# Transposing the second product of an MLP block, building a mask once, and loading the next stage earlier in a fused attention and two-MLP kernel

## The chip, the core and the metric

One NeuronCore of one Trainium2 chip runs the whole program. The metric is device time in microseconds (us), the median of three runs. The engines are TensorE (PE in the profile; its weight loads are a row of their own, PEld), VectorE (DVE), ScalarE (ACT), GpSimd (POOL) and SyncE (SP), which here issues nearly all transfers.

## The reference, cut to what matters

```python
# q, k, v: (4, 8, 576, 64); f: (4, 8, 576); per MLP: w_in (512, 2048), w_out (2048, 512); all float32
scores = q @ k.T / 8 + (cum[:, None] - cum[None, :])      # cum = cumsum(log(clip(f)))
x = softmax(causal(scores)) @ v                           # heads joined: x is (2304, 512)
h = x @ w_in;  y = (h - tanh(h)) @ w_out                  # first MLP
h = y @ w2_in; out = maximum(h, 0) ** 2 @ w2_out          # second MLP
```

## The kernel before

**Number format.** Each float32 operand of the MLPs is kept as two fp32r tiles, a rounded part ("hi", index 0) and the rest ("lo", index 1). A product is three matmuls, listed in `PASSES`: hi by hi, hi by lo, lo by hi. `ghl` is the pair for the activations between the layers, `wout(fc, hl, lo, n)` the pair for 128 rows of `w_out`, of which it gives columns `lo` to `lo + n`.

**Order.** A stream of attention steps and a stream of first-MLP steps are interleaved by cost (the `Clockwork` object runs each step, and runs follow-up work, such as a conversion, a set number of steps later). A scheduler then orders each engine's queue by that program order and by when it expects operands. From the last MLP block on, many instructions are held to program order (`pin`, `move`).

**Attention sums.** The cumulative sums of `log f` are matmuls with a triangle of ones. `first_sums` builds that triangle on POOL in a tile `early("tri")`, and makes the sums for the first 256 positions. At slot 16 of the attention `more_sums` builds the triangle again in a buffer of the ring "g" (three buffers, also used for the MLP's tanh results `g1` and for `ys`), copies a 64x64 corner of it twice (`twice`), makes the sums of the later positions, and builds a causal mask, of which `mask4` keeps two corners.

**First MLP.** 2304 tokens are taken in seven blocks of 256 tokens (j = 0 to 6) and one last block of 512 (j = 7, `LAST`). A block of 256 takes 8 steps, each with two 128-wide chunks of the hidden layer; the last block takes 16 steps with one chunk each. A step has the products into `h` (line 1010), then tanh on ACT (1020), the subtraction on DVE (1023), hi on ACT (1027) and lo on DVE (1031). One step later `y1_atoms` adds that chunk's part to y (line 1050): the weights are the stationary operand and the activations stream through, so y comes out transposed, 128 model dimensions by tokens. For a block of 256 each of the four atoms of a step writes one half of a PSUM bank, with matmuls 256 columns wide: 24 to a step. When a block is done, `y1_out` copies its two banks `y0` and `y1` into `ys` (the first on DVE, the second on ACT) and stores each with one transfer to `yscr[j]`, which is laid out `[128, 4, 256]`.

**Weights of the second MLP.** During the last block the second MLP's `w_in` is loaded in eight pieces (line 140), unpacked (ACT 203 and 204, DVE 210 and 212), combined into sums on POOL (256) and split into hi and lo (ACT 312, DVE 313). A piece can only be loaded when the last block has used the weights that lie in its place.

**First stage of the second MLP.** It works on 768 tokens at a time. Its first third of y is read back from `yscr` by `first_y_load` (12 transfers, line 151) at step 6 of the last block; at step 8 `y_sums` queues four subtractions on POOL (line 1178); at steps 9 to 15 `y_split` makes one of seven hi and lo pairs each (ACT 1166, DVE 1167). After the last block come its products (`r`, line 1222) and then the second layer (`o`, line 1380).

Of the kernel before, what the change touches and what calls it, by code (L numbers as in the profile page):

```python
# [10 lines left out]
F32 = mybir.dt.float32  # L11
# [99 lines left out]
def fused_kernel(ctx: ExitStack, tc: tile.TileContext, q, k, v, f, w1i, w1o, w2i, w2o, out):  # L111
# [269 lines left out]
    def early(name):  # L381
        return m1.tile([P, 2, 512], F32, tag="ghl", name=name, bufs=2).rearrange("p a n -> p (a n)")[:, :S]

    def triangle(tri):
        nc.gpsimd.memset(tri, 1.0)
        nc.gpsimd.affine_select(tri[:, 0:P], tri[:, 0:P], pattern=[[1, P]], compare_op=ALU.is_ge,
                                fill=0.0, base=0, channel_multiplier=-1)
# [25 lines left out]
            nc.vector.tensor_scalar(ccol[:, t], cps[:, t * 32 : t * 32 + 32], 8.0, None, op0=ALU.mult)  # L413

    def first_sums():
        flog = early("flog")[: B * H]
        load(flog, f.rearrange("b h s -> (b h) s"))
        load_next("qk")
        load_next("v")
        load_next("qk")  # L420
        load_next("v")
        feed.upload(UP[0])
        make_identity(nc, ident)
        tri = early("tri")
        triangle(tri)
        nc.vector.tensor_scalar(flog, flog, 1e-4, 1.0, op0=ALU.max, op1=ALU.min)
        nc.scalar.activation(flog, flog, AF.Ln)
        nc.scalar.activation(st[0][: B * H, :1], flog[:, :1], AF.Exp)
        lps = bank("a", 4, "lps")
        for c, (k0, kn) in enumerate(KC):  # L430
            nc.tensor.transpose(lps[:kn, c * 32 : c * 32 + 32], flog[:, k0 : k0 + kn], ident[:32, :32])
        nc.vector.tensor_copy(lfT[:, 0:4], lps[:, 0:128].rearrange("p (c h) -> p c h", c=4))
        nc.vector.tensor_copy(lfT[:64, 4], lps[:64, 128:160])
        t = bank("a", 4, "neg0")
        for i in range(2):
            for c in range(2):
                k0, kn = KC[c]
                nc.tensor.matmul(t[:, 256 * i + k0 : 256 * i + 256], lhsT=lfT[:, c, i : i + 1].to_broadcast([P, P]),
                                 rhs=tri[:, : 256 - k0], start=c == 0, stop=c == 1)
        neg = ap.tile([P, S], F32, tag="neg", name="neg_0", bufs=2)  # L440
        nc.scalar.activation(neg[:, :512], t, AF.Copy, scale=-8.0)
        for i in range(2):
            negs[i] = neg[:, 256 * i : 256 * i + 256]
        sum_logs(0, tri, flog)

    def more_sums():
        row = m1.tile([P, 512], F32, tag="g", name="row1", bufs=3)
        tri = m1.tile([P, 512], F32, tag="g", name="tri1", bufs=3)
        triangle(tri)
        t = m1.tile([P, 512], F32, tag="g", name="mask1", bufs=3)  # L450
        m, twice = t[:, :P], t[:D, P : 2 * P]
        for x in range(2):
            nc.gpsimd.tensor_copy(twice[:, x * D : x * D + D], tri[:D, :D])
        sum_logs(1, tri, row[: B * H], twice)
        nc.gpsimd.memset(m, 0.0)
        nc.gpsimd.affine_select(m, m, pattern=[[-1, P]], compare_op=ALU.is_ge, fill=MASK, base=0, channel_multiplier=1)
        for x in (slice(0, D), slice(D, P)):
            nc.gpsimd.tensor_copy(mask4[x], m[x, x])

    units = [(b, hf, h) for hf in range(2) for b in range(B) for h in range(H)]  # L460
    NU = len(units)
# [140 lines left out]
            cw.later(LAG['qk'], lambda: nc.vector.tensor_copy(kq(n), t))  # L602
        return [(1024, a)]

    KLh = []
# [30 lines left out]
    def k_split(n):  # L636
        if not KLh:
            open_halves()
        r = raws.pop(("qk", n))[:, :S]
        for i in range(2):  # L640
            own = slice(i * D, i * D + D)
            split(r[own], K1[own, i, :], KLh[i][own, :])
        nc.sync.dma_start(K1[D : 2 * D, 0].bitcast(F32), K1[0:D, 0].bitcast(F32))
        nc.sync.dma_start(K1[0:D, 1].bitcast(F32), K1[D : 2 * D, 1].bitcast(F32))

    def softmax_of(i):

# [77 lines left out]
    def s_atom(i):  # L725

        n, ts = slots[i]
        hh = units[n][2] % 2

        def a():  # L730
            ti, rows, o, w = ts[0]
            parts = []
            for c0, m in ((0, w),) if w <= 512 else ((0, 288), (288, 288)):
                t = bank("a", 4, f"s_{i}_{c0}")
                todo = [(h, xt(n, h, q_cols(h, 4) - D * (1 - h), P)) for h in (1, 0)] if ti == 4 else [(hh, xt(n, hh, q_cols(hh, ti), P))]
                for x, (h, lhsT) in enumerate(todo):
                    nc.tensor.matmul(t[:, :m], lhsT=lhsT, rhs=K1[:, h, c0 : c0 + m], start=x == 0, stop=False)  # L737
# [296 lines left out]
        return [(6 * n, lambda i=i: a(i)) for i in range(len(todo))]  # L1034

    def y1_atoms(j, s):
        n = 512 if j == LAST else NB
        per = 512 // n
        end = s == n_steps(j) - 1

        def a(i):
            if s == 0 and i == 0:
                yb[j] = [bank("a", 4, f"y1_{j}_{m}") if j == LAST else bank(f"y{m}", 1, f"y1_{j}_{m}")
                         for m in range(ND // per)]
            ghl = gt[j, s]
            t = yb[j][i // per]
            o = t[:, (i % per) * n : (i % per) * n + n]
            for fj, fc in enumerate(chunks_of(j, s)):
                for wh, xh in PASSES:
                    nc.tensor.matmul(o, lhsT=wout(fc, wh, i * P, P), rhs=ghl[:, xh, fj * n : fj * n + n],  # L1050
                                     start=s == 0 and fj == 0 and wh + xh == 0 and i % per == 0,
                                     stop=end and fj == per - 1 and wh == 1, skip_group_check=True)
            if end and i % per == per - 1:
                cw.later(1, lambda: y1_out(j, i // per))

        return [(3 * per * n, lambda i=i: a(i)) for i in range(ND)]

    def y1_out(j, m):
        ys = m1.tile([P, 512], F32, tag="g", name=f"ys_{j}_{m}", bufs=3)
        (nc.scalar.copy if m % 2 else nc.vector.tensor_copy)(ys, yb[j][m])  # L1060
        if j == LAST:
            for o in range(2):
                nc.sync.dma_start(yscr[j + o][:, m, :], ys[:, o * NB : (o + 1) * NB])
        else:
            nc.sync.dma_start(yscr[j][:, 2 * m : 2 * m + 2, :], ys.rearrange("p (c n) -> p c n", c=2))

    def mlp1_stream():

# [2 lines left out]
        for i, (j, s) in enumerate(steps):  # L1071
# [87 lines left out]
    def y_quarter(dst, i, dh, th):  # L1159
        for b in range(3):  # L1160
            move(dst[:, :, b * P : (b + 1) * P],
                 yscr[3 * i + b][:, 2 * dh : 2 * dh + 2, th * P : (th + 1) * P])

    def y_split(i, k, src):
        t = y_tile(i, k)
# [14 lines left out]
    def y_sums(i):  # L1180
        for x in range(4):
            cw.later(2 * x, lambda x=x: y_sum(i, x))

    def first_y_load():
        m2 = box2["m2"]
# [356 lines left out]
```

## Time and profile before

| | |
|---|---|
| Median of three runs | 1023.09 us (1022.45 to 1023.16) |
| Profiled execution | 1020.46 us, of which 1018.7 us are the span from the first to the last instruction |
| Mean granted TensorE clock | 0.991 of full speed |
| Start of the kernel and attention alone | up to about 55 us |
| Attention with blocks 0 to 6 of the first MLP | to 530 us; block 6 ends at 559 us |
| Last block of 512 tokens | 553 to 655 us |
| Second MLP, first layer and second layer | 655 to 860 us, and from there to the end |

The profile is of a single execution, and its span is 1.8 us shorter than the execution's own time. Times given as positions are microseconds from the first instruction.

### The profile page before, as it was taken

What the parts mean: (1) busy time and instruction counts of PE and PEld (TensorE: products, weight loads), DVE (VectorE), ACT (ScalarE), POOL (GpSimd) and SP (SyncE); (2) the same over time, 40 slices, a digit from 0 to 9 for tenths busy, and PEclk for the clock granted to TensorE, in tenths of its full rate; (3) what the DMA queues carried; (4) which work ended last, traced back from release to release, by engine and by line L of the source; (5) the groups of instructions that cost most, each with busy time, mean ns of one, the idle gap of its engine ahead of it and who ended that gap; (6) DMA issues with size and microseconds to landing.
All of it is one profiled execution on the core that took longest, in us unless ns stands there. A gap on an engine that the chain in (4) does not pass through costs nothing.

```text
span 1018.7 us, 19954 instructions
## 1 busy us (share of the span) xinstructions
PE 987.6 (97%) x7022; PEld 939.2 (92%) x7022; DVE 717.8 (70%) x1497; ACT 628.7 (62%) x1249; POOL 350.5 (34%) x515
## 2 busy tenths in 40 slices
PE   7989999999999999999999989999999998999998
PEld 5778889999999999999999867899999998999998
DVE  4895974677877777877653488855447579887773
ACT  5895974566666665765643357767667776655551
POOL 3673642455465555555420163352232000000000
PEclk9997999999999999999999999999999999999999
DMA  8937655253353443443201532385977975444431
GB/s 236 274 125 220 206 122 114 71 138 74 90 135 83 100 114 91 110 103 85 68 14 37 155 109 98 109 286 198 307 255 265 299 245 147 145 135 135 124 105 42
DMA packets 217445, 146.97 MB, mean 144 GB/s; under 512 B 115872, under 2 KB 195040, under 8 KB 217344
## 3 DMA queue, kind: packets, MB, share of 16 engines
q1 hardware_dynamic: 217296, 145.65, 49.0%
q8 instruction: 55, 0.90, 0.4%
q14 instruction: 46, 0.38, 0.1%
q10 hardware_dynamic: 48, 0.03, 0.0%
HBM read 101.00 MB, written 39.92 MB: 138 GB/s over the span
## 4 chain that ended last, share of the span: by engine, by line
PE 74%; DVE 8%; issue 6%; ACT 5%; POOL 3%; DMA 3%; SPq 0%; ACTq 0%; DVEq 0%; POOLq 0%
PE h L1010 16%; PE o L1380 15%; PE r L1222 15%; PE y L1050 15%; PE pv L855 4%; PE pt L772 2%; PE s L737 2%; PE s L738 2%; PE pv L817 1%; POOL Pb L549 1%; DVE ghl L1031 1%; DVE g L1023 1%; POOL w L228 1%; DMA wraw<-in_moe_w_in_dram 1%; PE s L706 1%
## 5 line engine op out<-in xcount | busy, mean ns | idle before, releaser
L1050 PE MATMUL y<-ghl,w 128*128 128x256 f32 (+1 forms) x1536 | 244.3, 303 | 4.6 <-DVE ghl L1031 4.6
L1050 PEld LDWEIGHTS y<-ghl,w 128*128 128x128 f32 x1536 | 211.6, 192 | 18.4 <-DVE ghl L1031 6.5
L1010 PE MATMUL h<-x,w 128*128 128x256 f32 x1344 | 196.2, 289 | 5.6 <-POOL w L228 5.1
L1010 PEld LDWEIGHTS h<-x,w 128*128 128x128 f32 x1344 | 175.1, 192 | 10.0 <-POOL w L228 6.6
L1380 PE MATMUL o<-ws,gc 128*128 128x256 f32 x864 | 116.4, 283 | 0.0
L1380 PEld LDWEIGHTS o<-ws,gc 128*128 128x128 f32 x864 | 109.3, 192 | 0.0
L1222 PE MATMUL r<-yt,ws 128*128 128x384 f32 x576 | 106.0, 336 | 1.0 <-ACT g L1240 1.0
L1222 PEld LDWEIGHTS r<-yt,ws 128*128 128x128 f32 x576 | 100.0, 188 | 2.7 <-ACT g L1240 2.3
L1380 PE MATMUL o<-wq,gc 128*128 128x256 f32 x648 | 91.6, 284 | 3.1 <-DVE gc L1346 2.5
L256 POOL TENSOR_TENSOR wsum<-wfull 128x256 f32<-128x256 f32 x32 | 31.0, 969 | 167.1 <-DVE wfull L212 139.5
L1380 PEld LDWEIGHTS o<-wq,gc 128*128 128x128 f32 x648 | 83.7, 192 | 4.0 <-DVE gc L1346 3.1
L691 POOL TENSOR_SCALAR Pb<-Pb,st 128x384 f32<-128x384 f32 (+2 forms) x80 | 53.8, 672 | 97.2 <-DVE st L685 81.6
L1346 DVE TENSOR_TENSOR gc<-graw,gc 128x1792 fp32r<-128x1792 f32 x34 | 68.6, 2022 | 20.1 <-ACT gc L1345 20.0
L675 ACT ACTIVATE Pb<-Pb,st 128x384 f32<-128x384 f32 (+2 forms) x80 | 55.2, 690 | 43.8 <-DVE st L666 42.6
L1222 PE MATMUL r<-yt,wq 128*128 128x384 f32 x432 | 80.0, 335 | 0.3 <-ACT g L1240 0.2
L1023 DVE TENSOR_TENSOR g<-h,g 128x512 f32<-128x512 f32 x72 | 49.4, 686 | 42.6 <-ACT g L1020 41.4
L666 DVE CUSTOM_DVE_ANT_0 Pb<-s,Pb 128x128 f32<-128x128 f32 (+4 forms) x144 | 66.7, 479 | 17.7 <-PE s L738 12.2
L1222 PEld LDWEIGHTS r<-yt,wq 128*128 128x128 f32 x432 | 75.1, 188 | 1.3 <-ACT g L1240 1.2
L1345 ACT ACTIVATE gc<-graw 128x1792 fp32r<-128x1792 f32 x34 | 57.7, 1699 | 29.6 <-PE o L1380 17.1
L1020 ACT ACTIVATE g<-h 128x512 f32<-128x512 f32 x72 | 42.5, 590 | 46.1 <-PE h L1010 43.4
L782 DVE TENSOR_TENSOR PT<-pt,PT 128x512 fp32r<-128x512 f32 (+1 forms) x80 | 50.7, 634 | 26.4 <-ACT PT L781 23.1
L1233 DVE TENSOR_TENSOR g<-r,g 128x384 f32<-128x384 f32 x71 | 39.1, 553 | 41.6 <-PE r L1222 23.4
(162 smaller groups left out, 1895.7 us busy)
## 6 DMA issues: line engine op xcount, KB each, us to landing
graw<-gscr SPq DMA_DIRECT2D x144, 128.0 KB, 2.5
gscr<-g SPq DMA_DIRECT2D x95, 192.0 KB, 4.4
wraw<-in_moe_w_in_dram SPq DMA_DIRECT2D x32, 512.0 KB, 4.6
wraw<-in_moe_w_out_dram SPq DMA_DIRECT2D x32, 512.0 KB, 5.5
neg<-cscr SPq DMA_DIRECT2D x32, 288.0 KB, 3.7
v<-in_v_dram SPq DMA_DIRECT2D x48, 128.0 KB, 2.8
qk<-in_k_dram SPq DMA_DIRECT2D x64, 72.0 KB, 2.4
K<-K SPq DMA_DIRECT2D x32, 144.0 KB, 3.3
```

Of the source, the lines that this page charges most:

```text
L666: nc.vector.tensor_tensor_reduce(out=d, in0=t[:rows, src : src + m], in1=d, scale=-0.125, scalar=3.0e38 if j == 0 else stat(0, x)[:rows], ...
L675: nc.scalar.activation(d, d, AF.Exp, bias=stat(len(parts) - 1, x)[:rows], scale=-1.0, accum_out=stat(2, x)[:rows])
L691: nc.gpsimd.tensor_scalar(d, d, r, 1.0, op0=ALU.mult, op1=ALU.mult)
L782: cw.later(LAG['trlo'], lambda: nc.vector.tensor_tensor(dst[1], src, dst[0].bitcast(F32), op=ALU.subtract))
L1010: nc.tensor.matmul(o, lhsT=win(fc, wh, dc), rhs=xpart(j, dc, xh), start=dc == 0 and wh + xh == 0, stop=dc == ND - 1 and wh == 1)
L1020: pin(nc.scalar.activation(g, t, AF.Tanh))
L1023: pin(nc.vector.tensor_tensor(g, t, g, op=ALU.subtract))
L1050: nc.tensor.matmul(o, lhsT=wout(fc, wh, i * P, P), rhs=ghl[:, xh, fj * n : fj * n + n], start=s == 0 and fj == 0 and wh + xh == 0 and i % ...
L1222: nc.tensor.matmul(t, lhsT=wprod(1, p, k, wh)[:, dc * P : (dc + 1) * P], rhs=yt[i, k][:, xh, dc], start=k in FRESH and dc == 0 and wh + xh ...
L1345: pin(nc.scalar.activation(hi, t[:, 1:8], AF.Copy))
L1346: pin(nc.vector.tensor_tensor(lo, in0=t[:, 1:8], in1=hi.bitcast(F32), op=ALU.subtract))
L1380: nc.tensor.matmul(o, lhsT=gc[n][gh, e][:, GWHERE[k]] if n == 1 else gc[n][gh][:, GWHERE[k], e], rhs=wprod(2, 2 * q + e, k, wh), start=q = ...
```

## The change

Three edits are made together. The triangle and the mask are built once, in `first_sums`, in the memory that the attention's K tiles take later; `more_sums` uses them again. The second product of the blocks of 256 has its operands exchanged: a 128-token piece of the activations is stationary and 512 columns of `w_out` stream, so that y comes out as tokens by model dimensions, in half as many matmuls of twice the width. Both banks are then transposed in blocks of 32 by 32 on DVE and stored by four transfers each, with 128-byte runs, into a `yscr` that is now laid out `[512, 256]`. The last block keeps its form. The load, the sums and the splits for the second MLP's first stage are spread from step 1 of the last block on.

```diff
-    yscr = [dram.tile([P, ND, NB], F32, name=f"yscr_{j}") for j in range(NBLK)]
+    yscr = [dram.tile([DM, NB], F32, name=f"yscr_{j}") for j in range(NBLK)]
...
-    K1 = ap.tile([P, 2, S], F32R, name="K1")
-    KL = ap.tile([P, S], F32R, name="KL")
+    K1, KLh = [], []
+    early = [ap.tile([P, 2, S], F32, tag="K1", name="early0", bufs=1),
+             ap.tile([P, S], F32, tag="KL", name="early1", bufs=1)]
...
     def first_sums():
-        flog = early("flog")[: B * H]
+        flog = early[0][: B * H, 1]
...
-        tri = early("tri")
+        tri = early[0][:, 0]
         triangle(tri)
+        m, twice = early[1][:, :P], early[1][:D, P : 2 * P]
+        for x in range(2):
+            nc.gpsimd.tensor_copy(twice[:, x * D : x * D + D], tri[:D, :D])
+        nc.gpsimd.memset(m, 0.0)
+        nc.gpsimd.affine_select(m, m, pattern=[[-1, P]], compare_op=ALU.is_ge, fill=MASK, base=0, channel_multiplier=1)
+        for x in (slice(0, D), slice(D, P)):
+            nc.gpsimd.tensor_copy(mask4[x], m[x, x])
...
     def more_sums():
-        row = m1.tile([P, 512], F32, tag="g", name="row1", bufs=3)
-        tri = m1.tile([P, 512], F32, tag="g", name="tri1", bufs=3)
-        triangle(tri)
...     (the same copies, mask and corners as above, in a third buffer of "g")
+        sum_logs(1, early[0][:, 0], early[0][: B * H, 1], early[1][:D, P : 2 * P])
...
     def open_halves():
-        KLh.append(KL)
+        K1.append(ap.tile([P, 2, S], F32R, tag="K1", name="K1", bufs=1))
+        KLh.append(ap.tile([P, S], F32R, tag="KL", name="KL", bufs=1))
...
     def y1_atoms(j, s):
...
+        todo = [(m, fj, fc) for m in range(len(yb0[j])) for fj, fc in enumerate(chunks)]
...
+            for x, y in PASSES:
+                if j == LAST:
+                    l, r = wout(fc, x, m * P, P), ghl[:, y]
+                else:
+                    l, r = ghl[:, x, fj * NB + m * P : fj * NB + m * P + P], wout(fc, y)
+                nc.tensor.matmul(o, lhsT=l, rhs=r, start=s == 0 and fj == 0 and x + y == 0,
+                                 stop=end and fj == len(chunks) - 1 and x == 1)
...
     def y1_out(j, m):
         ys = m1.tile([P, 512], F32, tag="g", name=f"ys_{j}_{m}", bufs=3)
-        (nc.scalar.copy if m % 2 else nc.vector.tensor_copy)(ys, yb[j][m])
...
-            nc.sync.dma_start(yscr[j][:, 2 * m : 2 * m + 2, :], ys.rearrange("p (c n) -> p c n", c=2))
+        nc.vector.transpose(ys, yb[j][m])
+        for a in range(0, P, 32):
+            dst = yscr[j][:, m * P + a : m * P + a + 32].rearrange("(b j) t -> j b t", j=32)
+            nc.sync.dma_start(dst, ys[a : a + 32].rearrange("j (b t) -> j b t", t=32))
...
     def mlp1_stream():
-            if last and s == 6:
+            if last and s == 1:
                 yield 0, first_y_load, j
-            if last and s == 8:
-                yield 0, (lambda: y_sums(0)), j
-            if last and 9 <= s < 9 + len(SPLITS):
-                yield 0, (lambda s=s: y_split(0, SPLITS[s - 9], yraw[0][SPLITS[s - 9]])), j
+            if last and s in SUMMED:
+                yield 0, (lambda x=SUMMED.index(s): y_sum(0, x)), j
+            if last and s in SPLIT:
+                yield 0, (lambda k=SPLITS[SPLIT.index(s)]: y_split(0, k, yraw[0][k])), j
...
+    SUMMED, SPLIT = (3, 4, 6, 7), (5, 6, 8, 9, 11, 13, 15)
```

## Rows read from the trace of the kernel before

**Rows 1.** The page, busy time of each engine and its share.

```profile
PE 987.6 (97%) x7022; PEld 939.2 (92%) x7022; DVE 717.8 (70%) x1497; ACT 628.7 (62%) x1249; POOL 350.5 (34%) x515
```

**Rows 2.** Windows: length, busy time per engine, clock, DMA share, GB/s.

```profile
55.00:93.00 38.00, 33.81 (x201) 29.82 (x202) 26.93 (x59) 26.07 (x63) 19.51 (x26) 0.82 0.49 154
...
130.00:230.00 100.00, 98.61 (x808) 96.09 (x808) 66.31 (x180) 58.28 (x147) 40.80 (x74) 1.00 0.46 110
...
430.00:530.00 100.00, 99.02 (x783) 96.89 (x782) 70.41 (x187) 59.18 (x133) 48.74 (x79) 1.00 0.29 75
...
591.20:607.20 16.00, 12.33 (x49) 9.74 (x48) 13.12 (x14) 6.99 (x13) 11.39 (x8) 0.92 0.20 66
607.20:655.00 47.80, 46.85 (x208) 38.45 (x207) 41.95 (x60) 32.45 (x59) 19.98 (x19) 0.99 0.28 93
```

**Rows 3.** The chain that ended last: start, length, what.

```profile
544.62 2.88 PE y L1050 x24
...
553.26 2.75 PE h L1010 x12
...
577.95 2.72 PE y L1050 x12
...
647.97 4.18 PE r L1222 x24
...
654.91 65.07 PE r L1222 x372
```

**Rows 4.** Groups by shape, 130 to 561 us.

```profile
L1050 PE MATMUL y<-ghl,w 128*128 128x256 f32 x1196 | 171.2, 287 | 0.0
...
L1060 ACT COPY ys<-y 128x512 f32<-128x512 f32 x7 | 4.1, 586 | 5.3 <-PE y L1050 5.3
```

**Rows 5.** Groups by shape, whole span.

```profile
L1050 PE MATMUL y<-ghl,w 128*128 128x256 f32 x1344 | 195.5, 289 | 0.0
...
L634 DVE STREAM_TRANSPOSE qk<-qk 128x576 f32<-128x576 f32 x16 | 12.3, 771 | 0.2
...
L622 DVE STREAM_TRANSPOSE qk<-qk 128x320 f32<-128x320 f32 x16 | 8.1, 505 | 0.8 <-DMA qk<-in_q_dram 0.7
```

**Rows 6.** Waits of TensorE's weight loads, 130 to 553 us: total, times, longest.

```profile
PEld pv L855 <- ACT PT L781: 5.3, 14, 0.9
```

**Rows 7.** Transfers by source: count, KB each, us to landing.

```profile
qk<-in_k_dram SPq DMA_DIRECT2D x64, 72.0 KB, 2.4
...
yscr<-ys SPq DMA_DIRECT2D x14, 256.0 KB, 2.1
```

**Rows 8.** Timeline of POOL at the start and around 75 us.

```profile
10.50 0.72 POOL L549 TENSOR_SCALAR Pb<-neg,ccol 128x128 f32<-128x128 f32 x2 [7.77 <-DVE ccol L413]
...
73.54 0.53 POOL L385 MEMSET tri<- 128x512 f32 x1
...
77.68 2.50 POOL L228 TENSOR_TENSOR w<-wfull,w 128x512 fp32r<-128x512 f32 x2
```

**Rows 9.** Timeline of PE around 75 us.

```profile
74.12 2.35 PE L401 MATMUL rps<-tri,lfT 128*32 128x320 f32 x10 [0.94 <-POOL tri L385]
...
79.00 1.22 PE L1010 MATMUL h<-x,w 128*128 128x256 f32 x4 [1.43 <-POOL w L228]
```

**Rows 10.** Timelines of DVE, POOL and PE, 594 to 607 us.

```profile
599.09 2.24 DVE L313 TENSOR_TENSOR ws<-wsum,ws 128x512 fp32r<-128x512 f32 x1 [1.22 <-ACT ws L312]
601.25 2.30 DVE L1031 TENSOR_TENSOR ghl<-g,ghl 128x512 fp32r<-128x512 f32 x1
603.47 0.68 DVE L313 TENSOR_TENSOR ws<-wsum,ws 128x512 fp32r<-128x512 f32 x1
...
595.14 7.85 POOL L1178 TENSOR_TENSOR yr<-yr,yr 128x768 f32<-128x768 f32 x4
...
603.60 3.81 PE L1050 MATMUL y<-ghl,w 128*128 128x512 f32 x10 [3.67 <-DVE ghl L1031]
```

**Rows 11.** Timeline of SP in the last block.

```profile
576.24 7.64 SPq L151 DMA_DIRECT2D yr<-yscr x12
```

More of the change, by code (lines that the diff above doesn't have):

```diff
@@ L374, in fused_kernel @@
     PT, X = [], []
-    K1 = ap.tile([P, 2, S], F32R, name="K1")
-    KL = ap.tile([P, S], F32R, name="KL")
+    K1, KLh = [], []
+    early = [ap.tile([P, 2, S], F32, tag="K1", name="early0", bufs=1),
+             ap.tile([P, S], F32, tag="KL", name="early1", bufs=1)]
     VH = ap.tile([P, 2, 5, 2, D], F32R, name="VH")
     negs = {}
-    def early(name):
-        return m1.tile([P, 2, 512], F32, tag="ghl", name=name, bufs=2).rearrange("p a n -> p (a n)")[:, :S]
     def triangle(tri):
@@ L446, in more_sums @@
     def more_sums():
-        row = m1.tile([P, 512], F32, tag="g", name="row1", bufs=3)
-        tri = m1.tile([P, 512], F32, tag="g", name="tri1", bufs=3)
-        triangle(tri)
[L450 to L458, printed above, removed]
+        sum_logs(1, early[0][:, 0], early[0][: B * H, 1], early[1][:D, P : 2 * P])
     units = [(b, hf, h) for hf in range(2) for b in range(B) for h in range(H)]
@@ L603, in kq_atom @@
         return [(1024, a)]
-    KLh = []
     def open_halves():
-        KLh.append(KL)
+        K1.append(ap.tile([P, 2, S], F32R, tag="K1", name="K1", bufs=1))
+        KLh.append(ap.tile([P, S], F32R, tag="KL", name="KL", bufs=1))
         KLh.append(wide("KLz", F32R)[:, :S])
@@ L641, in k_split @@
             own = slice(i * D, i * D + D)
-            split(r[own], K1[own, i, :], KLh[i][own, :])
-        nc.sync.dma_start(K1[D : 2 * D, 0].bitcast(F32), K1[0:D, 0].bitcast(F32))
-        nc.sync.dma_start(K1[0:D, 1].bitcast(F32), K1[D : 2 * D, 1].bitcast(F32))
+            split(r[own], K1[0][own, i, :], KLh[i][own, :])
+        nc.sync.dma_start(K1[0][D : 2 * D, 0].bitcast(F32), K1[0][0:D, 0].bitcast(F32))
+        nc.sync.dma_start(K1[0][0:D, 1].bitcast(F32), K1[0][D : 2 * D, 1].bitcast(F32))
     def softmax_of(i):
@@ L736, in a @@
                 for x, (h, lhsT) in enumerate(todo):
-                    nc.tensor.matmul(t[:, :m], lhsT=lhsT, rhs=K1[:, h, c0 : c0 + m], start=x == 0, stop=False)
+                    nc.tensor.matmul(t[:, :m], lhsT=lhsT, rhs=K1[0][:, h, c0 : c0 + m], start=x == 0, stop=False)
                     nc.tensor.matmul(t[:, :m], lhsT=lhsT, rhs=KLh[h][:, c0 : c0 + m], start=False, stop=x + 1 == len(todo))
@@ L1036, in y1_atoms @@
     def y1_atoms(j, s):
-        n = 512 if j == LAST else NB
-        per = 512 // n
+        chunks = chunks_of(j, s)
         end = s == n_steps(j) - 1
+        todo = [(m, fj, fc) for m in range(len(yb0[j])) for fj, fc in enumerate(chunks)]
         def a(i):
             if s == 0 and i == 0:
[L1043 to L1054, printed above, removed]
@@ L1056, in y1_atoms @@
-        return [(3 * per * n, lambda i=i: a(i)) for i in range(ND)]
+                yb[j] = [bank(*x, f"y1_{j}_{m}") for m, x in enumerate(yb0[j])]
+            m, fj, fc = todo[i]
+            ghl, o = gt[j, s], yb[j][m]
+            for x, y in PASSES:
[5 more added lines that the diff above has]
+                                 stop=end and fj == len(chunks) - 1 and x == 1)
@@ L1058, in y1_out @@
+            if end and fj == len(chunks) - 1:
+                cw.later(1, lambda: y1_out(j, m))
+        return [(3 * DM, lambda i=i: a(i)) for i in range(len(todo))]
+    yb0 = {j: [("a", 4)] * 4 if j == LAST else [("y0", 1), ("y1", 1)] for j, _ in mblocks}
     def y1_out(j, m):
         ys = m1.tile([P, 512], F32, tag="g", name=f"ys_{j}_{m}", bufs=3)
-        (nc.scalar.copy if m % 2 else nc.vector.tensor_copy)(ys, yb[j][m])
         if j == LAST:
+            (nc.scalar.copy if m % 2 else nc.vector.tensor_copy)(ys, yb[j][m])
@@ L1062, in y1_out @@
             for o in range(2):
-                nc.sync.dma_start(yscr[j + o][:, m, :], ys[:, o * NB : (o + 1) * NB])
-        else:
-            nc.sync.dma_start(yscr[j][:, 2 * m : 2 * m + 2, :], ys.rearrange("p (c n) -> p c n", c=2))
+                nc.sync.dma_start(yscr[j + o][m * P : (m + 1) * P, :], ys[:, o * NB : (o + 1) * NB])
+            return
+        nc.vector.transpose(ys, yb[j][m])
+        for a in range(0, P, 32):
+            dst = yscr[j][:, m * P + a : m * P + a + 32].rearrange("(b j) t -> j b t", j=32)
+            nc.sync.dma_start(dst, ys[a : a + 32].rearrange("j (b t) -> j b t", t=32))
@@ L1161, in y_quarter @@
             move(dst[:, :, b * P : (b + 1) * P],
-                 yscr[3 * i + b][:, 2 * dh : 2 * dh + 2, th * P : (th + 1) * P])
+                 yscr[3 * i + b][2 * dh * P : 2 * (dh + 1) * P, th * P : (th + 1) * P].rearrange("(c p) t -> p c t", p=P))
     def y_split(i, k, src):
@@ L1178, in y_sum @@
         pin(nc.gpsimd.tensor_tensor(r[o], in0=r[a], in1=r[b], op=ALU.subtract))
-    def y_sums(i):
-        for x in range(4):
-            cw.later(2 * x, lambda x=x: y_sum(i, x))
     def first_y_load():
```

## The prediction

> **What bounds the kernel now.** I read the page first: TensorE is busy for 97% of the span, the next engine for 70% [rows 1]. A share like that is only an upper end, because matmuls overlap in the trace, so I then cut the span into stages by windows, and looked in the chain of waits at how fast PE runs when nothing holds it.
>
> From 130 to 530 us PE is busy for 98.6 to 99.0 us of every 100, at full clock, with DVE at 66 and 70 in the two windows shown of four, and DMA under half [rows 2]. The largest named wait of its weight loads from 130 to 553 us sums to 5.3 us, 0.9 at most each [rows 6]. This stretch is bound by the number and width of the matmuls. The front, 55 to 93 us, is another matter: PE is busy for 33.8 of 38 us, at a mean clock of 0.82 [rows 2]. In the last block PE stands still once for long: from 591 to 607 us it is busy for 12.3 of 16 us, at a clock of 0.92 [rows 2]. From 654.9 us on PE runs for 65 us without a break [rows 3], so what the last block gains, the end gains too.
>
> **The change part by part.**
>
> *The exchanged product.* The undisturbed pace stands in the chain: 24 matmuls of 256 columns take 2.88 us, 12 of 512 columns 2.72 us [rows 3]. The columns are the same in number; the difference, 0.16 us, is 12 fixed costs of 13 ns. There are 1344 narrow matmuls [rows 5], which is 56 steps, so at most 56 x 0.16 = 9.0 us. Of them 1196 lie after 130 us [rows 4], 49.8 steps or 8.0 us; those before 130 us I count at nothing, since PE waits there for weights to be unpacked. Of the 8.0 I take 7.3, because some waits between attention and MLP work will stay where they are while PE gets faster. The ends are 0, if PE's pace is not what counts, and 9.0.
>
> The Trainium skill prices this otherwise: in "TensorE: Matmul & The Clock Gate", section "Back-to-back issue gap", a warm matmul costs its columns at 2.4 GHz plus 2.5 ns, whatever its width. As an estimate by that page, 672 fewer matmuls save 1.7 us, and the sum below would be some 5.5 us higher. The rows at both widths disagree with 2.5 ns, and I go by the rows.
>
> The evacuation: 14 transposes of 128x512 on DVE replace seven DVE copies and seven ACT copies. DVE transposes of 576 and 320 columns took 771 and 505 ns [rows 5], so 1.04 ns a column and about 0.70 us for 512; no row shows one that reads PSUM. ACT's copy took 586 ns and a DVE copy is near the transpose, so DVE gains seven times 0.7, 5 us in 430, where it is idle for about a third: hidden. What is not free is the queue. ACT's copies waited 5.3 us in all for y's second bank [rows 4]; this wait now stands in DVE's queue, with softmax and the `lo` conversions (line 1031) behind it, and PE waits for those. Below: nothing, above: 5.3 us. I take 0.3, since the old wait is under 0.8 us a bank and DVE's idle third can take it up.
>
> The stores: two transfers a block become eight, 42 more issues on SP, of 64 KB in runs of 128 bytes. The nearest row is the attention's load of k, also in 128-byte runs, 72 KB landing in 2.4 us; the old store took 2.1 [rows 7]. Four issues of about half a microsecond and 2.4 us make 4.4 us. Who waits? `ys` holds a buffer of the ring "g" of three, and the tanh of the next block's step 2 wants it, about two steps later. A step takes 430 us / 50, 8.6 us; even without attention two take 11.5. So it is hidden with 7 us to spare. I take nothing; the other end is a rival below. Sum for this edit: 7.3 - 0.3 = 7.0 us.
>
> *Triangle and mask once.* From 73.54 to 77.68 us POOL does nothing but build the triangle, the mask and their copies, and then takes up the weight subtraction (228) [rows 8]. PE waits 0.94 us for the triangle and 1.43 us for that subtraction [rows 9], 2.4 us together. The edit takes both away, and frees three buffers of "g". I take 2.0, since unpacking has other waits close behind. Upper end 4.1, the whole POOL stretch. The moved part, at most those 4.1 us, lands at the start, where POOL idles for 7.8 us before its first decay row at 10.50 [rows 8]: hidden; if DVE's operations on the way to the first sums were held up by it, about 1 us is lost, which is the lower end. The memory is given up before the K tiles need it.
>
> *The earlier first stage.* The last block runs from 553.26 to 654.91, 101.65 us [rows 3]. Its work at undisturbed pace is 16 steps of twice 2.72, block 6's last y at 2.88, and the 24 early products at 4.18: 94.1 us. So 7.6 us are lost, and that is all this edit can give. Most of it is one event. Four subtractions run back to back on POOL from 595.14 to 603.0, and in that time DVE operations with two SBUF inputs take 2.24 and 2.30 us where the next of the same shape takes 0.68; PE waits 3.67 us for the second of them, the `lo` of line 1031 [rows 10], and then runs at reduced clock for a while (0.92 over the window, which is 1.3 of 16 us) [rows 2]. With one subtraction at a step of its own (1.96 us each), DVE loses about 1.6 us once a step, at steps 3 and 4 when it is nearly idle, and at 6 and 7 beside unpacking. Three of the seven splits also leave the stretch from 607 to 655, where DVE is busy for 42.0 of 47.8 us [rows 2]. I take 5.0 us: the 3.7 and the 1.3 just worked out. The other 2.6 I leave in the block, as the price of the subtractions at steps 6 and 7 and of splits that still meet unpacking. Ends: 0 if DVE's delay is only moved, and 7.6.
>
> The load's 12 issues took 7.64 us of SP [rows 11]; now they come at about 560 us, right after block 6's eight stores, and ahead of the first weight pieces. A piece late by some 4 us is not late for anything, as its products come after 648 us.
>
> **Sum.** 1020.46 - 7.0 - 2.0 - 5.0 = 1006.5 us for the profiled execution. That execution was 2.6 us faster than the median of the runs shown, so against the median it is 1023.1 - 14.0 = 1009.1.
>
> **Rivals.**
>
> *PE is not the limit in the mixed stretch.* Softmax, transposes and P.V form a chain through DVE and ACT, and a faster y only makes PE wait in front of them. For it: the waits in rows 6 are all of that kind. Against: they are under 2% of the stretch. The first edit gives 0 to 2 us, the total is about 1015.
>
> *The last block's stall moves instead of going.* The sums at steps 6 and 7 now meet unpacking and the splits of steps 5 and 6 together, and `lo` is late there. For it: DVE's slow operations follow POOL wherever POOL runs. Against: four single delays have time between them. The third edit gives 0: 1014.
>
> *Slower: late stores hold the ring.* Writes of 128-byte runs are in no row. If a block's store lands later than about 17 us after its transpose (two steps), tanh waits for the `ys` buffer, then `ghl`, then PE. For it: sixteen times as many runs a block. Against: reads of the same runs land in 2.4 us, so a write would have to cost over six times as much. At 25 us the price is 8 us in each of six blocks, 48 in all, and the total 1057. The Trainium skill gives the rule behind this fear in "VectorE: DVE Perf Modes", section "The three transpose paths": a plain copy that transposes by strides is 19 times slower than the dedicated path. No run so far shows such a write; here only whole runs of 32 elements are strided, not single ones.
>
> *The small fixed cost* of the page cited above: 1014.6.
>
> **How the numbers follow.** My forecast has 0.62, the first rival 0.11, the second 0.11, the small fixed cost 0.02; all these are faster by over 0.2% (2.05 us, about what a measurement of this kernel can tell from no change): 0.86. The first two rivals together, or the DVE wait at its upper end on top of one of them, end near 1021 to 1024: 0.06 for no difference. Late stores: 0.08 for slower. All upper ends together (9.0 + 4.1 + 7.6) give 1002.4, so the range begins at 1002; it goes up to 1018, past each rival alone, and leaves out slower, no difference, and some 0.04 below. The likeliest is 1009.
>
> **What would show it.** Line 1050 with 672 matmuls of 512 columns in blocks 0 to 6, 12 in 2.72 us when undisturbed; the end of block 6 some 9 us earlier, of which 2 are there by 130 us; no POOL mask work at 75 us; no 3.7 us wait of line 1050 near 600 us, no clock dip there, and a last block of about 97 us; stores that land in 2 to 4 us. I am wrong if block 6 ends less than 5 us earlier, if the last block still takes over 100 us, or if tanh (line 1020) waits for a store.

## The result and the profile after

| | kernel before | changed kernel |
|---|---|---|
| Median | 1023.12 us (1022.45 to 1025.72) | 1034.74 us (1033.29 to 1036.19) |
| Ratio | | 1.0109, 95% interval 1.0083 to 1.0134 |
| Profiled execution, span | 1020.46, 1018.7 us | 1036.01, 1034.3 us |

The change made the kernel slower by 1.1%, where I had forecast 1.4% faster. I read the trace in the order of the stages, with the same views as before. The page's first row and the windows come first (length, then busy time and instructions of PE, PEld, DVE, ACT and POOL, mean granted clock, DMA share, GB/s):

```profile
PE 993.9 (96%) x6350; PEld 901.4 (87%) x6350; DVE 724.7 (70%) x1504; ACT 625.4 (60%) x1242; POOL 350.7 (34%) x513
```

```profile
10.50:55.00 44.50, 40.57 (x245) 30.69 (x244) 32.50 (x107) 32.45 (x92) 25.71 (x47) 0.96 0.91 262
55.00:93.00 38.00, 35.28 (x209) 28.36 (x209) 31.82 (x64) 28.80 (x69) 22.71 (x24) 0.91 0.52 162
93.00:130.00 37.00, 33.30 (x193) 28.45 (x192) 27.75 (x66) 27.18 (x67) 13.98 (x19) 0.86 0.61 185
...
130.00:230.00 100.00, 96.49 (x656) 84.90 (x653) 68.06 (x178) 59.35 (x146) 42.24 (x73) 1.00 0.46 106
230.00:330.00 100.00, 95.03 (x602) 84.83 (x603) 70.86 (x182) 56.90 (x129) 48.64 (x82) 0.98 0.40 91
330.00:430.00 100.00, 96.18 (x619) 85.58 (x618) 76.07 (x199) 59.06 (x139) 50.97 (x82) 1.00 0.39 89
430.00:530.00 100.00, 96.30 (x620) 84.57 (x619) 77.59 (x206) 60.84 (x141) 56.62 (x91) 1.00 0.44 100
573.80:670.70 96.90, 95.56 (x423) 78.11 (x422) 72.28 (x98) 54.58 (x97) 34.34 (x32) 1.00 0.36 111
```

Where the kernel before was full from 130 to 530 us [rows 2], PE now stands for 3.5 to 5 of every 100 us. By the positions at which `y0` is evacuated, block 0 ends at 151.2 us (before: 146.0) and block 6 at 578.0 (557.5). So 5.2 us are lost in the front and 15.3 in blocks 1 to 6. The last block, from 573.8 to 670.7, is 96.9 us long instead of 101.65 [rows 3]. From there to the end of the span both kernels take the same, 363.6 and 363.8 us.

Of the 5.2 us of the front the clock accounts for some 3.6, by an estimate. The time lost to it, (1 - clock) x length, sums to 10.4 us over the first three windows above; in the kernel before it is 6.8 us, 0.18 x 38 from 55 to 93 us [rows 2], with a clock of 1.00 in the other two. Part of this is a matter of the single execution: the kernels below that have the new front (and no held order in it) ended block 0 anywhere from 145.8 to 156.1 us, those with the old front from 145.5 to 148.6. Another part is not. From 93 to 130 us PE waits longer for the weight subtraction (total, times, longest; first the kernel before, then the changed one):

```profile
PE h L1010 <- POOL w L228: 0.5, 2, 0.3
```

```profile
PE h L1001 <- POOL w L228: 3.5, 2, 2.6
```

It is 2.1 to 3.5 us in every kernel below that has the first two edits and no held front, 1.6 in early_stage_and_mask, which has the first edit alone of the two, and 0.5 or 0.6 in those with the old front.

The new instructions themselves are as forecast. These are their groups, and the stores (count, KB each, median us to landing):

```profile
L1042 PE MATMUL y<-w,ghl 128*128 128x512 f32 x672 | 186.3, 408 | 0.3 <-DVE ghl L1022 0.3
...
L1059 DVE STREAM_TRANSPOSE ys<-y 128x512 f32<-128x512 f32 x14 | 9.9, 705 | 0.7 <-PE y L1042 0.6
```

```profile
yscr<-ys SPq DMA_DIRECT2D x56, 64.0 KB, 1.9
```

There are 672 wide matmuls. The transposes from PSUM take 705 ns (I had 0.70 us), and DVE waited 0.6 us for `y`, not 5.3. The stores of 128-byte runs land in 1.9 us, and in 4.7 at most. No tanh waits for one. PE's weight loads nevertheless wait longer (total, times, longest; 130 to 560 us; `pt` is attention's transposes of the probabilities, `PT` their converted result, `pv` its product with v):

```profile
PEld pv L846 <- ACT PT L772: 10.8, 22, 1.9
PEld pv L846 <- DVE PT L773: 4.9, 11, 0.8
PEld pt L758 <- POOL Pb L682: 4.4, 9, 0.7
PEld h L1001 <- ACT x L954: 3.6, 3, 1.8
PEld h L1001 <- DVE x L955: 2.5, 5, 0.9
```

The first was 5.3 us [rows 6]. The next views show what lies behind it, at the end of block 2. PE's timeline, then POOL's, then SP's:

```profile
295.08 1.15 PE L1001 MATMUL h<-x,w 128*128 128x256 f32 x5 [1.60 <-ACT x L954]
296.62 6.98 PE L1001 MATMUL h<-x,w 128*128 128x256 f32 x43 [0.40 <-DVE x L955]
303.44 0.87 PE L1042 MATMUL y<-w,ghl 128*128 128x512 f32 x3
304.15 0.34 PE L728 MATMUL s<-K,X 128*128 128x384 f32 x1
```

```profile
298.67 0.28 POOL L554 TENSOR_SCALAR_AFFINE_SELECT Pb<-Pb 128x128 f32<-128x128 f32 x1
307.68 0.59 POOL L682 TENSOR_SCALAR Pb<-Pb,st 128x384 f32<-128x384 f32 x1 [8.72 <-DVE st L676]
```

```profile
291.74 0.55 SPq L490 DMA_DIRECT2D qk<-in_q_dram  x1
297.99 6.70 SPq L1062 DMA_DIRECT2D yscr<-ys  x8
304.74 1.50 SPq L490 DMA_DIRECT2D qk<-in_q_dram  x3
```

PE does 48 matmuls of `h` in a row, the first products of two steps of the MLP, without one of attention between them. Softmax then has no scores to work on: POOL stands for 8.72 us. Before that, and after it, attention is bunched, and there PE waits for softmax results (the `pv` and `pt` waits above). In SP's queue one of four loads of q stands ahead of the eight stores and three behind them. In the kernel before, the place answering to it looks like this (windows of 6 us; first the kernel before, then the changed one):

```profile
285.00:291.00 6.00, 5.86 (x47) 5.62 (x46) 3.99 (x10) 3.73 (x9) 4.05 (x7) 1.00 0.82 227
```

```profile
297.00:303.00 6.00, 6.00 (x40) 5.99 (x39) 2.59 (x5) 1.23 (x2) 1.96 (x4) 0.72 0.27 46
```

PE is full in both, but in the second its mean granted clock is 0.72, and DVE, ACT and POOL are nearly idle. What they did not do then is missing later. One wait alone ends at a store, 0.6 us of ACT; the loss is in the order of PE's queue, which is fixed when the kernel is compiled. The next listing is worked out from that queue: each digit is attention's share, in tenths, of 12288 columns of matmuls, from about block 1 to block 6.

```
before   12332333242232333322332332233323233233224223233332233221
changed  12243300640730632322054153233300450540532006407206233221
```

### The profile page after: what moved, and what is told of

Same layout as the page of the kernel before. It is cut to its first block, busy times and chain, and to the rows that moved or that the text cites. A ratio compares the mean times of both kernels' runs of the same rounds, so it can differ in the third digit from the quotient of the medians.

```text
span 1034.3 us, 18600 instructions
## 1 busy us (share of the span) xinstructions
PE 993.9 (96%) x6350; PEld 901.4 (87%) x6350; DVE 724.7 (70%) x1504; ACT 625.4 (60%) x1242; POOL 350.7 (34%) x513
## 4 chain that ended last, share of the span: by engine, by line
PE 62%; DVE 9%; ACT 5%; issue 4%; DMA 3%; POOL 2%; SPq 1%; DVEq 0%; ACTq 0%; POOLq 0%
PE o L1374 15%; PE r L1216 14%; PE h L1001 13%; PE y L1042 11%; PE pv L846 2%; PE pt L763 2%; PE s L728 1%; PE s L729 1%; DVE PT L773 1%; DVE wq L313 1%; DVE Pb L657 1%; ACT PT L772 1%; POOL Pb L682 1%; DMA gscr<-g 1%; DVE ghl L1022 1%
## 5 line engine op out<-in xcount | busy, mean ns | idle before, releaser
L1001 PEld LDWEIGHTS h<-x,w 128*128 128x128 f32 x1344 | 178.3, 194 | 23.7 <-POOL w L228 8.5
L1042 PE MATMUL y<-w,ghl 128*128 128x512 f32 x672 | 186.3, 408 | 0.3 <-DVE ghl L1022 0.3
L1042 PEld LDWEIGHTS y<-w,ghl 128*128 128x128 f32 x672 | 122.6, 194 | 22.8 <-issue 2.0
L682 POOL TENSOR_SCALAR Pb<-Pb,st 128x384 f32<-128x384 f32 (+2 forms) x80 | 59.0, 739 | 76.5 <-DVE st L676 73.5
L1018 ACT ACTIVATE ghl<-g 128x512 fp32r<-128x512 f32 x72 | 45.4, 631 | 49.7 <-DVE g L1014 49.5
```

The lines of the kernel that those rows point to most:

```text
L682: nc.gpsimd.tensor_scalar(d, d, r, 1.0, op0=ALU.mult, op1=ALU.mult)
L1001: nc.tensor.matmul(o, lhsT=win(fc, wh, dc), rhs=xpart(j, dc, xh), start=dc == 0 and wh + xh == 0, stop=dc == ND - 1 and wh == 1)
L1018: pin(nc.scalar.activation(ghl[:, 0], g, AF.Copy))
L1042: nc.tensor.matmul(o, lhsT=l, rhs=r, start=s == 0 and fj == 0 and x + y == 0, stop=end and fj == len(chunks) - 1 and x == 1)
```

## The experiments

Theory 1: the compile-time scheduler takes the stores of 128-byte runs for slow, plans attention's loads late behind them, and so orders the queues in bunches; the chip, on which these stores are quick, has to run the bunched order. The rivals: the exchanged product or the transposes cost time themselves (theory 2), or the four issues for one on SP do (theory 3).

The kernel before ran beside each of them, with medians from 1022.1 to 1023.8 us. The last column is read from the one profiled execution of each, from the evacuation of `y0` of block 0 to that of block 6; it is 411.5 us in the kernel before and 426.8 in the changed one. product_only, four_long_stores, short_runs_only and all_with_long_runs leave out the right layout of the first MLP's result.

| Run | Median, us | Ratio to the kernel before, 95% interval | Blocks 1 to 6, us |
|---|---|---|---|
| product_only | 1018.33 | 0.9954 (0.9935 to 0.9973) | 406.2 |
| four_long_stores | 1020.14 | 0.9977 (0.9961 to 0.9992) | 408.5 |
| short_runs_only | 1041.37 | 1.0189 (1.0167 to 1.0210) | 429.9 |
| early_stage_only | 1018.59 | 0.9947 (0.9927 to 0.9967) | 411.5 |
| early_stage_and_mask | 1016.59 | 0.9927 (0.9901 to 0.9952) | 410.8 |
| all_with_long_runs | 1012.82 | 0.9901 (0.9874 to 0.9928) | 406.4 |
| held_order | 1025.91 | 1.0023 (1.0005 to 1.0040) | 415.2 |
| held_order_old_mask | 1025.68 | 1.0019 (1.0004 to 1.0034) | 412.2 |
| held_from_block_1 | 1020.62 | 0.9984 (0.9967 to 1.0000) | 414.2 |
| held_from_block_1_early_pt | 1019.90 | 0.9980 (0.9957 to 1.0003) | 415.9 |
| all_stores_from_act | 1022.41 | 0.9989 (0.9972 to 1.0007) | 415.0 |
| stores_from_act_spread | 1030.01 | 1.0073 (1.0050 to 1.0096) | 424.0 |
| stores_from_pool | 1075.62 | 1.0522 (1.0492 to 1.0551) | 464.7 |
| short_runs_when_read | 1040.80 | 1.0175 (1.0154 to 1.0196) | 406.2 |
| short_runs_read_reordered | 1042.87 | 1.0200 (1.0162 to 1.0238) | 406.2 |
| short_runs_read_later_sums | 1040.37 | 1.0165 (1.0137 to 1.0194) | 406.2 |
| short_runs_read_spread | 1036.27 | 1.0131 (1.0111 to 1.0152) | 406.3 |

**Which part of the exchanged product's edit costs.** Three kernels take it apart; the other two edits are left out of all three.

```diff
 # product_only
         nc.vector.transpose(ys, yb[j][m])
-        for a in range(0, P, 32):   # four stores, 128-byte runs
+        nc.sync.dma_start(rows, ys.rearrange("p (c n) -> p c n", c=2))   # one, 1 KB runs (the kernel before: one, 2 KB)
 # four_long_stores
+        for a in range(0, P, 32):   # four stores, 1 KB runs
+            nc.sync.dma_start(rows[a : a + 32], ys[a : a + 32].rearrange("p (c n) -> p c n", c=2))
 # short_runs_only: the old y1_atoms and the old copies of y; the new stores
```

> The exchanged product and the transpose of y on DVE, but each ys stored with one transfer in runs of 1 KB, as before (so the first MLP's result lies in the wrong layout for what follows); no early mask, no earlier first stage. Theory 1, the order: the scheduler takes stores of 128-byte runs for slow, lets attention's loads come late behind them and puts attention's matmuls off into bunches; PE then waits on the softmax chain. Without these runs the order is as even as before and the 13 ns a matmul show: 1023.1 - 7 = 1016 us. Theory 2, the product: the exchanged matmuls or the transposes in DVE's queue are themselves what costs the 20 us between 150 and 580 us: about 1040 us. Theory 3, SP: four issues instead of one hold up attention's loads in SP's queue on the chip: 1016 us here, as theory 1.

> As product_only, but each ys stored by four transfers of 32 partitions in runs of 1 KB (wrong layout again): as many issues as in the changed kernel, without its short runs. Theory 1 (order, by the price of short runs): 1016 us, as product_only. Theory 2 (product, transposes): about 1040 us. Theory 3 (issues on SP): about as slow as the changed kernel's stretch, 1035 to 1040 us.

> The old product and the old copies of y; only the stores are the new ones, four for each ys with 128-byte runs (wrong layout); nothing else of the change. Theory 1 (order): attention bunched and PE waiting, without the gain of the wide matmuls: 1036 to 1046 us. Theory 2 (product, transposes): no change, 1022 to 1025 us. Theory 3 (issues on SP): as theory 1, 1036 to 1046 us.

The short runs alone make the kernel 1.9% slower (19 us), with the old product and no transpose, so theory 2 falls. Four stores with long runs cost nothing like it, so theory 3 falls as well; a small cost of the issues is not excluded, since the intervals of product_only and four_long_stores overlap and blocks 1 to 6 take 2.3 us longer in the second. The compiled order of the long-run kernels is as even as before, and that of short_runs_only is bunched:

```
product_only      12332333242232333322332332233323233233224223233332233221
four_long_stores  12332333242232331422332332233323233233223323233332233221
short_runs_only   12332302614332432322062152233300730630531007307225333221
```

In the trace of short_runs_only PE stands as in the changed kernel; in that of product_only it is as full as before:

```profile
230.00:330.00 100.00, 95.02 (x732) 92.11 (x731) 71.04 (x181) 56.53 (x128) 48.09 (x80) 0.98 0.42 92
```

```profile
130.00:230.00 100.00, 98.83 (x679) 89.30 (x680) 68.28 (x186) 58.32 (x147) 41.16 (x75) 1.00 0.47 110
230.00:330.00 100.00, 98.39 (x647) 89.03 (x646) 78.69 (x204) 63.12 (x145) 54.62 (x91) 1.00 0.42 99
330.00:430.00 100.00, 99.31 (x663) 91.02 (x662) 82.31 (x217) 64.83 (x151) 56.34 (x91) 1.00 0.45 105
430.00:530.00 100.00, 99.26 (x653) 90.01 (x653) 69.25 (x182) 57.69 (x129) 45.77 (x74) 1.00 0.28 68
```

A reader can take the price of the order from the counts in parentheses: product_only has 679 + 647 + 663 + 653 = 2642 matmuls in these 400 us and the changed kernel, with the same kinds of matmuls, 656 + 602 + 619 + 620 = 2497. 400 x (1 - 2497 / 2642) = 22 us. The busy times differ by only 11.8 us. The last column of the table agrees with the counts: blocks 1 to 6 take 20.6 us more in the changed kernel than in product_only.

**The terms of the prediction, each alone and together.** early_stage_only has the earlier first stage alone, early_stage_and_mask that and the triangle and mask built once, and all_with_long_runs all three edits, with the store of product_only. Their code is that of the change.

> Only the third edit: the second MLP's first stage loaded, summed and split from step 1 of the last block on. By the prediction's term, 5.0 us: 1018.5 us, the last block 97 us long instead of 101.7. If the stall only moves: 1023.5.

> The first and third edits, without the exchanged product and its stores. Compiled order even as before. If the mask built once gains 2.0: 1016.5 us; if it gains nothing: 1018.5; if it costs what block 0 was late: 1022 to 1023.

> All three edits, but each ys stored with one transfer in runs of 1 KB (so the first MLP's result lies in the wrong layout); compiled order even. If the three gains add up as measured alone (5.4 product, 4.9 early stage, 2.0 mask): 1023.4 - 12.3 = 1011 us. If one eats another: 1014 or more.

The earlier first stage gains 5.4 us by the ratio (3.4 to 7.5). The mask adds 2.0 us by the medians, within the intervals. All three together, with long runs, gain 10.1 us (7.4 to 12.9), where 4.7 for the product, 5.4 and 2.0 make 12.1: the terms add up within the interval.

**The same stores, another order.** PE's attention and first-MLP matmuls are held to program order; the stores stay as the change has them, on SP.

```diff
+    def held(ins):
+        if steady:          # held_from_block_1: from block 1's first step on
+            tc.keep_in_program_order(ins)
...
-                nc.tensor.matmul(o, lhsT=l, rhs=r, start=...)
+                held(nc.tensor.matmul(o, lhsT=l, rhs=r, start=...))
```

> The whole change, stores as they are, with PE's attention and first-MLP matmuls held to program order from the time that the first MLP's weights are loaded. The compiled order is then as even as before. Theory 1 (only the order is wrong): the sum of what was measured alone, 1023.5 less 5.4 for the product and 4.9 for the earlier first stage, less 2 or more 2 for the mask built once: 1011 to 1015 us. Rival, the stores themselves (short runs or four issues cost time on the chip, or hold the ring): 1025 us or more. Rival, a fixed order makes PE wait for operands that it used to step around: 1020 us or more, with waits spread over the stretch.

> As held_order, but without the first edit: triangle and mask are built twice as before. If building them once gains the 2.0 us of the prediction: 2 us more than held_order. If it costs (the changed kernel and all_stores_from_act, which have it, were some 4 to 5 us late at block 0): up to 5 us less. If the lateness was that of single executions: the same within 1.5 us.

> As held_order, but PE's order is held only from block 1 on, so that the front is as in the changed kernel. held_order was late by some 9 us at block 0 and then level with the kernel before. If the held front was what it lost: 1015 to 1019 us. If program order costs in every block (waits of P.V for the converted probabilities): 1021 us or more.

The compiled order of held_from_block_1 is even again:

```
held_from_block_1 12332333332232333322332332233323233233233223233332233221
```

This order takes some 13 us off the changed kernel (1034.74 to 1020.62 by the medians, 12.8 by the ratios, 12.6 in blocks 1 to 6), although all 56 stores have their short runs and land in 1.9 us, as before. It does not reach 1012.8. Holding the front as well costs another 4 to 5 us (held_order against held_from_block_1, by ratios and medians), and from block 1 on PE waits longer for P.V's operand (weight loads of held_from_block_1, 130 to 560 us; product_only has 6.3 and 3.4 us in these rows):

```profile
PEld pv L851 <- ACT PT L777: 13.7, 16, 1.7
PEld pv L851 <- DVE PT L778: 3.7, 7, 0.9
```

So both halves of my expectation were too simple: most of the loss goes with the order, and some of it stays. These waits are 7.7 us more than in product_only, and blocks 1 to 6 take 8.0 us more. That this is the price of a fixed order is likely and not shown: no run holds the order with long runs, so a part of it may belong to the stores. The old mask made no difference here. I tried whether those waits come from the place of one conversion (`LAG` of `tr` 3 to 2):

> As held_from_block_1, with the conversion of the transposed probabilities one step of the stream earlier (a lag of 2 instead of 3). If P.V's 13.7 us of waits for it come from its place in ACT's queue: they fall by half or more and the time to 1012 to 1017 us. If ACT is simply behind: the same 1019 to 1022.

They did not fall (16.1 us), and the time did not change.

**The same stores from another queue.** Each kernel is the whole change with the stores issued elsewhere.

```diff
-            nc.sync.dma_start(dst, ys[a : a + 32]...)
+            nc.scalar.dma_start(dst, ys[a : a + 32]...)                # all_stores_from_act
+            cw.later(1 + a // 16 + m, lambda a=a: put(a))   # put() on nc.scalar: stores_from_act_spread
+                                                            # put() on nc.gpsimd: stores_from_pool
```

> The whole change, with one word altered: the stores of 128-byte runs are issued from ACT's queue instead of SP's, where attention's loads are. The order of PE is then nearly even. Theory 1 (order): the three gains of the prediction come out, less ACT's time for 56 issues, which I put at 0 to 3 us: 1009 to 1014 us. Theory 2 (product, transposes): 1030 to 1036 us. Theory 3 (issues on SP): 1009 to 1014 us.

> As all_stores_from_act, where eight issues in a row held ACT for 6 us at the end of a block, but spread over some four steps of the stream, so that ACT is held in pieces of some 0.7 us. If ACT's stop was what ate the gain there (7 blocks of up to 6 us, some of it in PE's way): 1015 to 1018 us. If the uneven places left in its order were: 1021 to 1023.

> The whole change, its stores of 128-byte runs issued from POOL's queue and spread over some four steps of the interleaved stream; the compiled order is within a few tenths of the even one. Theory 1 (only the order): 1011 us plus up to 4 us for POOL's time on 56 issues. Rival, short runs cost time on the chip whoever issues them: 1020 us or more.

From ACT the loss against the kernel before is gone, but the gain is not there. The timeline of ACT at the end of block 2 shows one reason:

```profile
291.43 6.01 ACTq L1062 DMA_DIRECT2D yscr<-ys  x8
297.48 0.72 ACT L666 ACTIVATE Pb<-Pb,st 128x512 f32<-128x512 f32 x1 [6.37 <-DMA yscr<-ys]
```

Eight issues in a row hold softmax back for 6 us. Another reason may be the order, which was not as even as I had expected: attention's share falls to 0 or 1 tenth in four places, and it does so in the spread kernel too:

```
all_stores_from_act    12332153242232320632332332230443233233221523233332232321
stores_from_act_spread 12332143242232320542332332230435233233221523233332232321
```

Spreading the issues made it worse, against both of my numbers. The holes are much the same, so they don't explain it. Once ACT stands for long behind a store (waits of ACT, 130 to 570 us); what else makes the 1030 us stays open.

```profile
ACT Pb L666 <- DMA yscr<-ys: 8.3, 1, 8.3
```

From POOL the compiled order is nearly even, and the kernel is slowest by far. Its timeline, and the largest wait of PE from 130 to 570 us:

```profile
169.94 0.65 POOL L1062 DMA_DIRECT2D yscr<-ys  x1 [4.27 <-issue]
172.38 0.66 POOL L1062 DMA_DIRECT2D yscr<-ys  x1 [1.80 <-issue]
174.84 0.65 POOL L1062 DMA_DIRECT2D yscr<-ys  x1 [1.80 <-PE pv L808]
```

```profile
PE pt L763 <- POOL Pb L682: 20.8, 5, 8.1
```

The issues follow each other at 2.45 us, of which only 0.65 is recorded as busy. If all 56 take that long, they hold POOL for 56 x 2.45 = 137 us, and attention's scaling (L682) is queued behind them. An even order is needed, and is not enough.

**The short runs on the reading side.** The whole change, with `ys` stored by one transfer in 512-byte runs, and read back in 128-byte runs.

```diff
-        for a in range(0, P, 32): ...
+        nc.sync.dma_start(yscr[j][m], ys.rearrange("p (c n) -> p c n", c=ND))   # yscr[j]: [2, ND, P, P]
...
+            src = yscr[j][th, 2 * dh : 2 * dh + 2].rearrange("c (a j) (q t) -> q j (c a) t", j=32, t=32)
+            for x in range(4):
+                move(to[32 * x : 32 * x + 32].rearrange("j (e t) -> j e t", t=32), src[x])
```

> The whole change, but each ys stored with one transfer in runs of 512 bytes, and the 128-byte runs moved to the reading side: a quarter of a block is read back by four transfers of 32 partitions instead of one, 48 for the first stage instead of 12. The compiled order of the mixed stretch is even. If only the order was at fault: as all_with_long_runs, 1012.8 us, plus what 36 more issues cost on SP in the last block. If 24 to 30 us of issues on SP make the first sums late: the last block some 5 to 10 us longer, 1018 to 1023 us.

> As short_runs_when_read, with the two quarters that the first sum wants read first. Half of the loads are then enough for it, 12 to 15 us after the first issue: 1011 to 1016 us. If the loads are not late for anything: the same as short_runs_when_read within 1.5 us.

> As short_runs_read_reordered, with the four sums and the first four splits one step (6 us) later. If the sums waited for the loads: 1 to 4 us less than short_runs_read_reordered. If not, the sums meet the unpacking of the second MLP's weights again: up to 4 us more.

> As short_runs_when_read, but the 48 loads of the first stage are issued one or two at a time over five steps of the last block, between the loads of the weights (the two quarters that the first sum wants go first; sums at steps 5 to 8, splits from 6 on), and those of the later stages three at a time. There the 48 loads in a row held SP for 24.45 us, the first weight piece behind them. If SP's queue was the whole loss in the last block and at 650 to 700 us: as all_with_long_runs within 3 us, 1011 to 1016. If the short reads are late whatever the queue: 1025 or more.

The mixed stretch came out as hoped: PE is busy for 394.5 of the 400 us from 130 to 530, as in all_with_long_runs (394.9), and blocks 1 to 6 take the 406.2 us of product_only. The loss is later. SP's timeline in the last block of short_runs_when_read, and PE's:

```profile
559.15 24.45 SPq L151 DMA_DIRECT2D yr<-yscr  x48
583.70 65.80 SPq L140 DMA_DIRECT2D wraw<-in_moe_w_in_dram  x16
```

```profile
590.76 0.79 PE L1001 MATMUL h<-xl,w 128*128 128x512 f32 x1 [8.40 <-DVE g L1014]
```

The weights' loads start 20 us later than in all_with_long_runs (563.38), and PE stands for 8.4 us, and later once for 9.5 us in the second MLP's first layer, for ACT. Neither the order of the reads nor the time of the sums matters. Spread out, 4 us come back, not 20 or more: the same wait is 3.7 us, and the waits of the second MLP's first layer for ACT are 6.9 us in all, 13 times. What makes those was not found. The fastest kernel here that computes the whole reference is early_stage_and_mask: 0.7% faster than the kernel before and 1.8% than the changed one (1016.59 / 1034.74 = 0.9825).

## Why the prediction was wrong

**The step that failed** is in the part on the exchanged product: "Who waits? [...] So it is hidden with 7 us to spare. I take nothing". The stores were priced by what they do on the chip, and there the price was right: 1.9 us to landing, no wait on the ring, no tanh late. They cost about 22 us all the same (1034.74 less 1012.82 of all_with_long_runs), because their form changes the order in which the scheduler lays out the queues for six blocks. My whole sum took it for granted that PE's queue stays as it was with new durations in it. Shown are three things: run length and not the number of stores switches the order (four_long_stores is even with as many, all_with_long_runs with the other edits), the bunched order goes with the loss even without the rest of the change (short_runs_only), and another order with the same stores on the same queue takes some 13 us of it away (held_from_block_1). What the last 8 us of held_from_block_1 are stays open. What the scheduler reckons for a short run does not stand in any trace; that it reckons more than the chip takes is concluded.

**The exchanged product** was right in kind and too large in size: 7.0 forecast, 4.7 by the ratio (2.8 to 6.6), and 5.3 in blocks 1 to 6 by the traces (411.5 less 406.2). Waits of P.V's weight loads took up some of it, 9.7 us against 7.9 before. This also bears on the fixed cost of a matmul. The Trainium skill, "TensorE: Matmul & The Clock Gate", section "Back-to-back issue gap", gives a warm matmul 2.5 ns over its columns, for an isolated one; by that figure 672 fewer matmuls would save an estimated 1.7 us. The interval of product_only lies above that.

**Triangle and mask once** had 2.0 us. The medians give 2.0 in one pair (early_stage_only and early_stage_and_mask) and nothing in another (held_order and held_order_old_mask), all within the intervals. In the trace PE's wait for the triangle is gone, and so is the mask's work at 75 us [rows 8, 9]. But the wait for the weight subtraction did not go, as I had forecast; it moved. From 55 to 93 us it fell from 2.8 to 1.6 us and the triangle's 0.9 us went; from 93 to 130 us it grew from 0.5 us to 3.5. Together these waits are 4.2 us in the kernel before, 5.1 in the changed one, and 2.8 in early_stage_and_mask. So alone the edit may gain what I forecast, though no interval shows it; beside the exchanged product PE's waits leave nothing of it.

**The earlier first stage** was right: 5.0 forecast, 5.4 measured (3.4 to 7.5). The last block was forecast at about 97 us and took 96.9. One detail was not as forecast: the four subtractions ran in two pairs (3.76 us from 591.88 us and 3.85 from 605.39), not one at a step. The stall of 3.67 us [rows 10] is gone, the clock from 573.8 to 670.7 us is 1.00, and PE's only named wait there is this (total, times, longest):

```profile
PE y L1042 <- DVE ghl L1022: 1.3, 2, 0.8
```

The chain in its second half runs at the undisturbed pace of [rows 3]:

```profile
652.61 2.72 PE h L1001 x12
655.33 2.72 PE y L1042 x12
```

**The rivals.** "Late stores hold the ring" put the loss at the right edit by the wrong mechanism: its condition, a landing later than 17 us, was missed by far. The page that I had cited for that fear, the Trainium skill's "VectorE: DVE Perf Modes", section "The three transpose paths", gives 19 times for a DMA copy that transposes by strides; no run here shows that: with whole runs of 32 elements 64 KB landed in 1.9 us, where 256 KB in long runs took 2.1 [rows 7]. "PE is not the limit in the mixed stretch" is false for the even order, where the product's gain is measured. For the bunched order it is open: there blocks 1 to 6 take 426.8 us with the wide matmuls and 429.9 with the narrow ones (short_runs_only), one execution each.

## What to carry to other kernels

Where a scheduler lays out the queues, an edit has two prices: what its instructions take on the chip, and what the scheduler's plan makes of them. Compare the compiled order of the two kernels before adding up durations, above all when a transfer changes its shape and shares a queue with loads that something else waits for. And when a bound engine is full in a window while the engines that feed its next work are idle, look for the loss in the windows after it.

## What the runs showed of the hardware

Stores of 64 KB landed in 1.9 us in 128-byte runs and in 1.7 us in 1 KB runs (four_long_stores). The short ones took SP 0.49 us each to issue; from ACT they held its queue for 6.01 us for eight, and from POOL they followed each other at 2.45 us. Executions of one kernel spread widely: the kernel before took 1019.5 to 1027.1 us in those made beside these runs, so that a position in the front of one profile (the clock from 93 to 130 us was 0.86 here, 1.00 in product_only) says little of an edit by itself. A wait that recurs in every profile, as that for the weight subtraction from 93 to 130 us, says more.
